# Six more products of a zero tile among the first value products of an mLSTM kernel

## The chip, the cores and the metric

The kernel runs on one core of a Trainium2 chip. The metric is the device time of one execution in microseconds (us). Three executions of the kernel before gave 563.04 us as median, from 562.67 to 563.28.

## The reference

Two parts follow each other. The first is an mLSTM recurrence over 768 positions for 4 batches and 8 heads of width 40, with an input gate, a forget gate, an output gate and a running maximum `m`:

```
m_new  = max(f[t] + m, i[t])
C      = exp(f[t] + m - m_new) * C + exp(i[t] - m_new) * outer(v[t], k[t])
n      = exp(f[t] + m - m_new) * n + exp(i[t] - m_new) * k[t]
y[t]   = sigmoid(o[t]) * (C @ q[t]) / max(|n . q[t]|, 1)
```

The second is a bilinear layer on the 3072 resulting rows of 320: `((y @ w_a) * (y @ w_b)) @ w_out`, with an inner width of 1536. The result is a float32 array of 3072 by 320.

## The kernel before, in words

The recurrence is computed in chunks of 128 positions. There are 24 pieces of attention work, 6 chunks for each of 4 batches; the program numbers them 0 to 23, and the numbers 0 to 3 are the first chunk of each batch. "Chunk 0" and "chunk 1" in the words on this change are the pieces 0 and 1. For one piece TensorE transposes q and k (L870), multiplies them (`pS`, L884), VectorE multiplies that by a matrix of decays (`gbc`, L890), TensorE multiplies the result by the values (`pV`, L927) and, for the state that the next chunk needs, weighted values by keys (`pU`, L628). VectorE then normalizes (`den`, `osig`, L669 to L680), TensorE transposes the result (`pX`, L707), and ScalarE and VectorE split it in a high and a low part, `xh` and `xl` (L711, L712). Those are the operands of the bilinear layer (`pu`, L810, and `pd`, L781), which is most of TensorE's work.

The weights arrive as 64 bit numbers and pass through 32 stages of preparation, each with a step on ScalarE (`signs`, L412), three on VectorE (`words`, L423, L424, L426), one on ScalarE (`leading`, L439), two small products (`pc`, L449 and L450) and one or two more steps on VectorE (`rests`, L457 or L455).

The opening of the kernel is written out by hand in `start()`, and every engine's order there is pinned to the order in which the code stands. From the end of `start()` on, a scheduler with its own timing model orders the instructions of each engine. In both parts each engine works its list off in order: an instruction that waits holds up all behind it on that engine.

In `start()` the function `busy(count)` issues `count` products of a tile of zeros, 128x336 in bf16 (L959), into a PSUM tile named `warm` that nobody reads. The opening has 13 of them at the very start, two at a time between the first steps, and groups of 4, 4, 4, 4 and 8 after the first update of the state. A function `dense` (L152) places three such products in front of the small products of the pieces 2 and 3. The groups after the state's update write a second tile, `warm2`, in the PSUM bank with the tag `pd2`; the first tile lies in the bank `pd1`, which the value product of piece 1 takes over.

Around the change, the order in `start()` is: the last product of the weights' stage 1 (`rests(1)`), `begin_c(0)` (the 8 heads' value products of piece 0), `weigh(0)` on GpSimd's side of the list, `signs(2)` on ScalarE, `begin_c(1)` (the value products of piece 1), `stage_f(0)`, `words(2)`, `stage_u(0)`.

Of the kernel before, what the change touches and what calls it, by code (L numbers as in the profile page):

```python
# [8 lines left out]
F32 = mybir.dt.float32  # L9
# [11 lines left out]
def kernel(  # L21
# [16 lines left out]
    P = 128  # L38
# [20 lines left out]
    ps_dn = ctx.enter_context(tc.tile_pool(name="ps_dn", bufs=1, space=PSUM))  # L59
# [89 lines left out]
    def dense(n, bank, count):  # L149
        if NS <= n < NE:  # L150
            for _ in range(count):
                nc.tensor.matmul(bank[:, 0:H * DV], zero[:, 0:P], zero, start=True, stop=True)  # L152
# [26 lines left out]
    def nat(n):  # L179
        return inner.get(n) or (qk[n % NQ], va[n % NQ])  # L180


    def load_qk(n):
        c, b = chunks[n]
        for j, x in enumerate((q, k)):
            issued["qk"[j], n] = nc.sync.dma_start(
                nat(n)[0][j][:, :, 0:D], x[b, :, c * P:(c + 1) * P, :].rearrange("h t d -> t h d")
            ).ins

    def load_v(n):  # L190
        c, b = chunks[n]
        nc.sync.dma_start(
            nat(n)[1][:, :, 0:D], v[b, :, c * P:(c + 1) * P, :].rearrange("h t d -> t h d")
        )

    def load(n):
        load_qk(n)
        load_v(n)
# [15 lines left out]
    def gate_o(c, bs=slice(0, B)):  # L214
        hot[0] = 3
        x = osig[c][:, bs, 0:DM]
        nc.scalar.activation(x, x, AF.Sigmoid)
# [16 lines left out]
    def gates_load():  # L234
        f, i = (apool.tile([P, S], F32, tag="pb", name=f"g_{x}")[0:BH] for x in "fi")
        nc.sync.dma_start(f, f_gate.rearrange("b h s -> (b h) s"))
        nc.scalar.dma_start(i, i_gate.rearrange("b h s -> (b h) s"))
        return f, i
# [136 lines left out]
    def fetch(to):  # L375
        while fetched[0] < min(to, len(stages)):
            x = fetched[0]
            fetched[0] += 1
            src = stages[x]
            n = src[0].shape[1]  # L380
            raw = rpool.tile([P, n], I64, tag=f"s{x}", name=f"raw{x}")
            r0 = 0
            for a in src:
                nc.sync.dma_start(raw[r0:r0 + a.shape[0]], a)
                r0 += a.shape[0]
            held[x] = [raw, n]
# [9 lines left out]
    def turn(j, x):  # L396

        if begun[j] > x:
            return False
        assert begun[j] == x  # L400
        begun[j] += 1
        return True

    def signs(x):
        if not turn(0, x):
            return
        raw, n = held[x]
        t = step[x % len(step)][:, :n]
        words = raw.bitcast(U32).rearrange("p (n w) -> p n w", w=2)
        held[x] += [t, words[:, :, 0]]  # L410
        with tc.issue_after(rounded[x - 2]) if x > 4 else nullcontext():
            nc.scalar.activation(  # L412
                t, words[:, :, 1].bitcast(F32), AF.Prelu, scale=2.0 ** -112, alpha=-(2.0 ** 32)
            )
# [16 lines left out]
    def leading(x):  # L431
        if not turn(2, x):
            return
        n, W, r = held[x]
        w = ws[x] = rpool.tile([P, 2, n], F32R, tag=f"s{x - 1}", name=f"w{x}")
        h = w[:, 0]
        if len(stages[x]) > 1:
            h = cpool.tile([P, WCH], F32R, tag="ct", name="ct", bufs=2)
        rounded[x] = nc.scalar.copy(h, W).ins  # L439
        held[x] += [w, h]  # L440

    def rests(x):
        leading(x)
        if not turn(3, x):
            return
        ready[0] = x + 1
        n, W, r, w, h = held.pop(x)
        pc = ps_up.tile([P, NTB], F32, tag="pu", name=f"pc{x}")[:, :n]
        nc.tensor.matmul(pc, eye[0], r, start=True, stop=False)  # L449
        nc.tensor.matmul(pc, eye[1], h, start=False, stop=True)  # L450
        if len(stages[x]) > 1:
            for j in range(2):
                rows, other = (slice(64 * i, 64 * i + 64) for i in (j, 1 - j))
                nc.scalar.copy(w[rows, j], W[rows])
                nc.vector.tensor_tensor(w[other, j], pc[rows], W[rows], op=ALU.add)  # L455
        else:
            nc.vector.tensor_tensor(w[:, 1], pc, W, op=ALU.add)  # L457
# [124 lines left out]
    def weigh(n):  # L582
        c, b = chunks[n]
        vw = apool.tile([P, H, DV], F32, tag="vw", name=f"vw{n}", bufs=1)
        nc.gpsimd.tensor_tensor(  # L585
            vw, nat(n)[1], w_col(c, b).unsqueeze(2).broadcast_to([P, H, DV]), op=ALU.mult
        )
        vws[n] = vw
# [326 lines left out]
    def begin_c(n):  # L915
        c, b = chunks[n]
        s = st[n]
        if n >= NS:
            weigh(n)
        if n < NS:  # L920
            pV = ps_dn.tile([P, 512], F32, tag=f"pd{min(n, 2)}", name=f"pV{n}")
        else:
            pV = ps_at.tile([P, 512], F32, tag="pat", name=f"pV{n}")
        pv = pV[:, 0:H * DV].rearrange("p (h d) -> p h d", h=H)
        dense(n, pV, 3)
        for h in range(H):
            nc.tensor.matmul(pv[:, h], s["E"][:, h, :], nat(n)[1][:, h], start=True, stop=True)  # L927
            if h % HH == HH - 1:
                yield
        if c > 0:  # L930
            nc.vector.tensor_tensor(s["num"], pv, s["num"], op=ALU.add)
        else:
            s["num"] = pv
        yield
# [14 lines left out]
    with tc.tile_pool(name="spool", bufs=3) as spool:  # L949

        def room(name):
            return spool.tile([P, H * P], F32, tag="x", name=name)

        def start():
            warm = ps_dn.tile([P, 512], F32, tag="pd1", name="warm")

            def busy(count):
                for _ in range(count):
                    nc.tensor.matmul(  # L959
                        warm[:, 0:H * DV], zero[:, 0:P], zero, start=True, stop=True  # L960
                    )

            def run(x, count=99):
                for _ in range(count):
                    if next(x, "end") == "end":
                        return

            busy(13)
            f, i = gates_load()
            load_qk(0)  # L970
            load_qk(1)
            fetch(2)
            load_v(0)
            load_v(1)
            fetch(3)
            load_o(0, (0, 1))
            fetch(5)
            load_qk(NS)
            load_o(0, (2, 3))
            fetch(6)  # L980
            load_v(NS)
            fetch(8)
            load(NS + 1)
            fetch(12)
            m0, w = gates_first(f, i)
            rest = gates_rest(f, i, m0)
            a0, e0, b0, e1, b1 = begin_a(0), begin_e(0), begin_b(0), begin_e(1), begin_b(1)
            run(a0, 1)
            busy(2)
            run(a0)  # L990
            busy(2)
            run(b0, 1)
            busy(2)
            run(rest, 1)
            signs(0)
            run(e0)
            words(0)
            run(begin_a(1))
            leading(0)
            signs(1)  # L1000
            run(b0)
            run(e1)
            gates_w(w)
            words(1)
            rests(0)
            run(b1)
            leading(1)
            gate_o(0, slice(0, 2))
            rests(1)
            run(begin_c(0))  # L1010
            weigh(0)
            signs(2)
            run(begin_c(1))
            run(stage_f(0))
            words(2)
            run(stage_u(0))
            load(NS + 2)
            weigh(1)
            leading(2)
            signs(3)  # L1020
            run(stage_f(1))
            d0, d1 = stage_d(0), stage_d(1)
            warm = ps_dn.tile([P, 512], F32, tag="pd2", name="warm2")
            busy(4)
            run(d0, 1)
            words(3)
            run(d0)
            leading(3)
            busy(4)
            rests(2)  # L1030
            signs(4)
            run(stage_u(1))
            fetch(18)
            load(NS + 3)
            fetch(26)
            busy(4)
            run(d1, 1)
            words(4)
            run(d1)
            leading(4)  # L1040
            busy(4)
            rests(3)
            busy(8)
            rests(4)
            signs(5)
            gate_o(0, slice(2, B))
            words(5)
            return rest

        with in_order():  # L1050
            rest = start()
# [66 lines left out]
```

## Time and profile before

| | |
|---|---|
| median of the executions timed | 563.04 us (562.67 to 563.28) |
| profiled execution: its own time | 560.51 us |
| its span, first to last instruction | 558.5 us |
| mean granted TensorE clock | 0.993 |
| busy: TensorE / VectorE / ScalarE / GpSimd | 544.9 / 389.4 / 267.9 / 126.9 us |

PE is TensorE's multiplying, PEld its loading of weights, DVE is VectorE, ACT ScalarE, POOL GpSimd and SP the queue that issues the transfers. A row of the timeline shows the start, the length up to the end of the last instruction merged in it, the engine, the line, the operation, the tiles and shapes and the number of instructions; in brackets stands how long the engine had been idle, and what ended that. Since matmuls are pipelined, the length of a row runs over the start of the next, and the time that a group takes is read from its start to the start of the next group. A fp32 product counts as two instructions. PEclk is the share of TensorE's full clock that was granted.

### The profile page before, as it was taken

To read this page: it belongs to the slowest core of one execution; us is meant where nothing else is said; L and a number is where in the kernel's file an instruction comes from. 1 tells how busy PE (TensorE), PEld (TensorE's weight loads), DVE (VectorE), ACT (ScalarE), POOL (GpSimd) and SP (SyncE) were. 2 spreads that over 40 slices of the span, in tenths; PEclk is the share of its full clock that TensorE was granted. 3 is DMA by queue.
4 is the path that set the end of the run, shared out by engine and by line. 5 is a ranking of instruction groups with operands and counts; after the bars stand their busy time and mean duration, and the time that the engine had idled before them with its cause. 6 is when DMAs were issued, how large, how long until landed. Compare 5 with 4: busy or idle time off the path is not lost.

```text
span 558.5 us, 12726 instructions
## 1 busy us (share of the span) xinstructions
PE 544.9 (98%) x4925; PEld 518.0 (93%) x4925; DVE 389.4 (70%) x888; ACT 267.9 (48%) x645; POOL 126.9 (23%) x188
## 2 busy tenths in 40 slices
PE   8999999899999999999999999999999999999997
PEld 6898898799999899999989999998999999999997
DVE  6889999964858683968749774977757755944332
ACT  5574678752626761556525654644526733310111
POOL 3102414641232320332031330333021302000000
PEclk9799999999999999999999999999999999999999
DMA  9999941393649762569536684586539704200001
GB/s 191 215 263 291 290 72 51 94 179 71 108 103 193 141 139 58 123 142 180 107 99 156 108 151 115 118 145 138 118 97 154 144 0 115 48 1 25 0 1 35
DMA packets 198551, 66.75 MB, mean 120 GB/s; under 512 B 184220, under 2 KB 191772, under 8 KB 198492
## 3 DMA queue, kind: packets, MB, share of 16 engines
q1 hardware_dynamic: 198444, 65.86, 56.4%
q8 instruction: 38, 0.62, 0.5%
q14 instruction: 21, 0.17, 0.1%
q10 hardware_dynamic: 48, 0.10, 0.0%
HBM read 41.11 MB, written 5.95 MB: 84 GB/s over the span
## 4 chain that ended last, share of the span: by engine, by line
PE 60%; DMA 17%; DVE 10%; ACT 5%; issue 3%; SPq 3%; POOL 1%; ACTq 0%; DVEq 0%; POOLq 0%
PE pu L810 31%; PE pd L781 15%; DMA T<-qks 4%; DMA c_dram<-cb 3%; ACT gbc L490 3%; DMA va<-in_v_dram 2%; PE pV L603 2%; PE pU L628 2%; DVE gbc L554 2%; DMA gbc<-g_dram 1%; DMA raw<-in_moe_w_a_dram 1%; DVE pb L556 1%; PE pS L884 1%; PE pV L927 1%; PE pS L545 1%
## 5 line engine op out<-in xcount | busy, mean ns | idle before, releaser
L810 PE MATMUL pu<-xh,w 128*128 128x384 f32 (+1 forms) x1080 | 276.5, 324 | 2.6 <-ACT g L816 0.9
L810 PE MATMUL pu<-xl,w 128*128 128x384 f32 (+1 forms) x648 | 208.0, 322 | 0.0
L810 PEld LDWEIGHTS pu<-xh,w 128*128 128x128 f32 x1080 | 190.6, 189 | 5.9 <-ACT g L816 1.3
L781 PE MATMUL pd<-w,gh 128*128 128x320 f32 x576 | 126.7, 309 | 0.0
L810 PEld LDWEIGHTS pu<-xl,w 128*128 128x128 f32 x648 | 122.2, 189 | 0.2
L817 DVE TENSOR_TENSOR g<-pu,g 128x384 f32<-128x384 f32 (+1 forms) x108 | 54.6, 505 | 89.4 <-PE pu L810 46.3
L781 PEld LDWEIGHTS pd<-w,gh 128*128 128x128 f32 x576 | 96.7, 188 | 0.1
L781 PE MATMUL pd<-w,gl 128*128 128x320 f32 x288 | 85.3, 310 | 0.0
L816 ACT COPY g<-pu 128x384 f32<-128x384 f32 (+1 forms) x90 | 39.6, 440 | 93.4 <-PE pu L810 84.2
L490 ACT ACTIVATE gbc<-gbc,gtab 128x128 f32<-128x128 f32 x160 | 49.1, 389 | 18.1 <-POOL gbc L483 18.0
L821 DVE TENSOR_TENSOR gl<-g,gh 128x384 fp32r<-128x384 f32 (+1 forms) x92 | 52.2, 568 | 1.9
L781 PEld LDWEIGHTS pd<-w,gl 128*128 128x128 f32 x288 | 53.1, 188 | 0.2
L585 POOL TENSOR_TENSOR vw<-va,gtab 128x336 f32<-128x336 f32 x20 | 16.4, 822 | 160.3 <-PE pU L628 135.2
L819 DVE CAST gh<-g 128x384 fp32r<-128x384 f32 (+1 forms) x108 | 41.1, 382 | 2.2
L483 POOL TENSOR_SCALAR_AFFINE_SELECT gbc<-gbc 128x1024 f32<-128x1024 f32 x20 | 22.6, 1132 | 65.1 <-DMA gbc<-g_dram 32.9
L554 DVE TENSOR_TENSOR gbc<-gbc,pb 128x512 f32<-128x512 f32 x36 | 27.2, 757 | 6.8 <-ACT pb L552 6.6
L603 PEld LDWEIGHTS <-pb 128*128 128x128 bf16 x576 | 23.4, 96 | 6.4 <-DVE pb L556 3.2
L684 POOL TENSOR_TENSOR osig<-osig,den 128x320 f32<-128x320 f32 x22 | 16.6, 754 | 54.9 <-DVE den L671 42.9
L603 PE MATMUL pV<-va,pb 128*128 128x42 bf16 x288 | 25.9, 183 | 2.7 <-DVE pb L556 2.7
L790 ACT COPY o<-pd 128x320 f32<-128x320 f32 x24 | 8.8, 434 | 40.3 <-PE pd L781 40.3
L550 DVE TENSOR_TENSOR gbc<-pS,gbc 128x512 f32<-128x512 f32 x36 | 23.7, 682 | 4.0 <-PE pS L545 4.0
L518 ACT COPY qks<-qks 128x640 bf16<-128x640 bf16 x36 | 26.0, 725 | 0.6
(154 smaller groups left out, 849.6 us busy)
## 6 DMA issues: line engine op xcount, KB each, us to landing
gbc<-g_dram SPq DMA_DIRECT2D x20, 512.0 KB
q<-in_q_dram SPq DMA_DIRECT2D x24, 160.0 KB
k<-in_k_dram SPq DMA_DIRECT2D x24, 160.0 KB
va<-in_v_dram SPq DMA_DIRECT2D x24, 160.0 KB
osig<-in_o_gate_dram SPq DMA_DIRECT2D x24, 160.0 KB
raw<-in_moe_w_out_dram SPq DMA_DIRECT2D x12, 320.0 KB
out_dram<-o SPq DMA_DIRECT2D x24, 160.0 KB
raw<-in_moe_w_a_dram SPq DMA_DIRECT2D x8, 384.0 KB
```

The source lines that it names most:

```text
L483: nc.gpsimd.affine_select(E, E, pattern=[[0, H], [1, P]], compare_op=ALU.is_ge, fill=-1e30, base=0, channel_multiplier=-1,)
L490: nc.scalar.activation(E[:, h], E[:, h], AF.Exp, bias=beta[:, h:h + 1])
L518: nc.scalar.copy(qks[:, 0, :, lo:lo + 2 * D], qks[:, 1, :, D - lo:3 * D - lo])
L550: nc.vector.tensor_tensor(E, pS, E, op=ALU.mult)
L554: nc.vector.tensor_tensor(E, E, pb[:, 0], op=ALU.subtract)
L603: nc.tensor.matmul(pv[:, h], pb[i][:, h % HH, :], vb[j][:, h], start=(x == 0), stop=(x == len(terms) - 1),)
L781: nc.tensor.matmul(pd[t][:, 0:DM], a[:, cols], w, start=(ff == 0 and first), stop=(ff == NF - 1 and last),)
L810: nc.tensor.matmul(acc[j], a, r, start=(x == 0), stop=(x == len(terms) - 1),)
L816: (nc.vector.tensor_copy if ff in [1, 2] else nc.scalar.copy)(g, acc[0])
L817: nc.vector.tensor_tensor(g, acc[1], g, op=ALU.mult)
L819: nc.vector.tensor_copy(gh, g)
L821: (nc.gpsimd if kb * 12 + ff < 16 else nc.vector).tensor_tensor(gl, g, gh.bitcast(F32), op=ALU.subtract)
```

## The change

The tile `warm2` is allocated earlier in `start()`, right after `rests(1)`. Two zero products are added in front of the value products of piece 0, and four between `signs(2)` and the value products of piece 1. All groups of zero products that were there stay.

```diff
@@ -1007,9 +1007,12 @@
             leading(1)
             gate_o(0, slice(0, 2))
             rests(1)
+            warm = ps_dn.tile([P, 512], F32, tag="pd2", name="warm2")
+            busy(2)
             run(begin_c(0))
             weigh(0)
             signs(2)
+            busy(4)
             run(begin_c(1))
             run(stage_f(0))
             words(2)
@@ -1020,7 +1023,6 @@
             signs(3)
             run(stage_f(1))
             d0, d1 = stage_d(0), stage_d(1)
-            warm = ps_dn.tile([P, 512], F32, tag="pd2", name="warm2")
             busy(4)
             run(d0, 1)
             words(3)
```

The first place is TensorE's list in `start()`, from the products of the weights' stage 1 (`pc`) to the state's update of piece 0 (`pU`). Before:

```order
L449 MATMUL pc_371<-cr,eye_80 128x384
L450 MATMUL pc_371<-w_368,eye_81 128x384
L927 MATMUL pV_375<-va_88,gbc_265 128x42 x8
L927 MATMUL pV_387<-va_89,gbc_317 128x42 x8
L628 MATMUL pU_407<-vw_384,k_85 64x42 x8
```

With the change (the two rows on `zero` and `warm_375` stand once for the first two products, and once for the four):

```order
L449 MATMUL pc_371<-cr,eye_80 128x384
L450 MATMUL pc_371<-w_368,eye_81 128x384
L959 LDWEIGHTS zero
L959 MATMUL warm_375<-zero 128x336
...
L927 MATMUL pV_378<-va_88,gbc_265 128x42 x8
L959 LDWEIGHTS zero
L959 MATMUL warm_375<-zero 128x336
...
L927 MATMUL pV_394<-va_89,gbc_317 128x42 x8
L628 MATMUL pU_414<-vw_387,k_85 64x42 x8
```

Nothing else moves in `start()`, on TensorE or on another engine. The scheduler's part stands as before at first, and from some 67 us of the span to some 155 us the engines' lists differ by places that were swapped. The second place is the first such swap on TensorE, around the products `pS` and `pI` of piece 5, which share two PSUM banks. Before:

```order
L450 MATMUL pc_982<-w_980,eye_81 128x320
L884 MATMUL pS_1_1121<-T_0_992,T_1_1012 128x128 x4
L449 MATMUL pc_1035<-cr,eye_80 128x384
L450 MATMUL pc_1035<-w_1033,eye_81 128x384
L781 MATMUL pd_0_578<-w_908,gh_3_938 128x320 x2
```

With the change:

```order
L450 MATMUL pc_988<-w_986,eye_81 128x320
L781 MATMUL pd_0_584<-w_914,gh_3_944 128x320 x2
L781 MATMUL pd_1_585<-w_914,gh_3_944 128x320 x2
L884 MATMUL pS_1_1127<-T_0_998,T_1_1018 128x128 x4
L904 MATMUL pI_0_1182<-cst_96,T_0_998 128x42 x4
L781 MATMUL pd_0_584<-w_914,gl_3_946 128x320
```

The first half of `pI`, which stood behind 16 products `pu` and four `pd` groups, now follows `pS` directly. VectorE's list moves with it: the multiplication L890, which empties the banks of `pS`, stands seven rows (first half) and three rows (second half) nearer to the front.

## The prediction

> **What bounds the kernel now.** I read the page first. TensorE is busy for 544.9 of 558.5 us, so what counts is how fast it works. One row of the 40 slices shows the only place where its clock gives way:
>
> ```profile
> PEclk9799999999999999999999999999999999999999
> ```
>
> The second slice (14 to 28 us) has 7 tenths. The view of windows finds the edges:
>
> ```profile
> 15.24:18.65 3.41, 3.41 (x33) 3.41 (x31) 2.86 (x9) 2.46 (x3) 0.00 (x0) 1.00 0.89 196
> 18.65:22.06 3.41, 3.41 (x26) 2.81 (x26) 3.20 (x10) 1.47 (x5) 0.75 (x1) 0.50 1.53 158
> 22.06:25.47 3.41, 3.41 (x24) 2.52 (x23) 2.69 (x7) 1.53 (x4) 0.00 (x0) 0.50 1.07 294
> 25.50:26.00 0.50, 0.50 (x7) 0.36 (x6) 0.47 (x2) 0.23 (x1) 0.13 (x1) 1.00 1.10 289
> ```
>
> Column three is PE, the number behind the last bracket is the clock. It is 1.00 up to 18.65, exactly half for 6.82 us, and full again. PE was never idle in it. The timeline of PE over that place, which is also the chain of waits there:
>
> ```profile
> 15.37 3.90 PE L927 MATMUL pV<-va,gbc 128*128 128x42 f32 x32
> 19.20 1.54 PE L628 MATMUL pU<-vw,k 128*64 128x42 f32 x16
> 20.67 1.30 PE L959 MATMUL warm<-zero 128*128 128x336 bf16 x4
> 21.77 0.85 PE L707 MATMUL pX<-ident,osig 128*128 128x128 f32 x3
> 22.41 1.33 PE L959 MATMUL warm<-zero 128*128 128x336 bf16 x4
> 23.32 0.73 PE L449 MATMUL pc<-cr,eye 128*128 128x384 f32 x1
> 23.85 0.52 PE L450 MATMUL pc<-w,eye 128*128 128x384 f32 x1
> 24.30 1.43 PE L628 MATMUL pU<-vw,k 128*64 128x42 f32 x16
> 25.66 0.74 PE L959 MATMUL warm<-zero 128*128 128x336 bf16 x4
> 26.24 0.49 PE L707 MATMUL pX<-ident,osig 128*128 128x128 f32 x3
> 26.57 0.73 PE L959 MATMUL warm<-zero 128*128 128x336 bf16 x4
> 27.02 0.45 PE L449 MATMUL pc<-cr,eye 128*128 128x384 f32 x1
> 27.32 0.34 PE L450 MATMUL pc<-w,eye 128*128 128x384 f32 x1
> 27.50 1.31 PE L959 MATMUL warm<-zero 128*128 128x336 bf16 x8
> 28.65 0.60 PE L870 MATMUL pT<-ident,q 128*128 128x128 f32 x4
> ```
>
> No row has a bracket: PE waits for nobody, its own work sets the pace. The clock falls after 3.3 us of value products, which stream only 42 columns each.
>
> **What the half clock costs.** The same operations at full clock, from start to next start, stand partly above and partly here:
>
> ```profile
> 40.38 1.88 PE L927 MATMUL pV<-va,gbc 128*128 128x42 f32 x16
> 42.09 0.36 PE L810 MATMUL pu<-xh,w 128*128 128x256 f32 x1
> 78.54 0.92 PE L628 MATMUL pU<-vw,k 128*64 128x42 f32 x16
> 79.39 0.38 PE L810 MATMUL pu<-xh,w 128*128 128x256 f32 x1
> ```
>
> pV x16 takes 1.71 and pU x16 0.85. A zero product takes 0.144 (eight from 27.50 to 28.65), the four of 25.66 took 0.58, pX 0.33 (26.24 to 26.57), pc 0.48 (27.02 to 27.50). Between 15.37 and 25.66 that makes, half clock against full: pV 3.83 against 3.42, pU 1.47 against 0.85, four zeros 1.10 against 0.58, pX 0.64 against 0.33, four zeros 0.91 against 0.58, pc 0.98 against 0.48, pU 1.36 against 0.85. The differences, 0.41, 0.62, 0.52, 0.31, 0.33, 0.50 and 0.51, sum to 3.20 us. The six added products cost 6 x 0.144 = 0.86 on the same path. Net -2.34: pT would start at 26.3 instead of 28.65.
>
> **Does the clock hold?** The trace does not show the new sequence, so I bound it by columns streamed in 3.41 us. From 15.24 to 18.65 PE ran 31 value products of 42 columns and one pc of 384, some 1690 columns, and the clock fell at the end. The poorest stretch that I found elsewhere in which it held is this one, the page's busy row and the part of it that is pV of a later piece:
>
> ```profile
> 189.31:192.72 3.41, 2.55 (x67) 2.34 (x66) 3.38 (x9) 1.66 (x4) 0.04 (x1) 1.00 0.77 173
> 189.31:192.72 3.41, 1.55 (x48) 1.34 (x48) 1.00 0.77 173
> ```
>
> 48 x 42 and, of the other 19, sixteen pU of 42 and about one pu of 384 make some 3070 columns, with PE idle for 0.86, at clock 1.00. In the changed kernel 15.24 to 18.65 holds the pc, six zeros (2016) and 2.41 us of value products at 0.107 (22 x 42), some 3320; the next 3.41 us hold eight zeros and the rest. That is above the stretch that held. If the 3.41 us were laid worst, with only four zeros in them, it is 1344 + 26 x 42 = 2440, half way between the two. So I take full clock as the value; both ends stay in the range: all of the 3.20 saved, or nothing of it.
>
> The Trainium skill, "TensorE: Matmul & The Clock Gate", section "What's actually happening", says that a monitor looks at how busy the array was in free-running windows of 3413 ns and passes full or half clock. The 6.82 us here are two of those. Its section on HAM oscillation asks for no idle gaps of over some 3 us; taken by that alone the clock would not have fallen here, where PE had no gap at all, and zeros would only cost their 0.86. The trace speaks against that reading.
>
> **What hides or stops the gain.** Earlier PE work must find its inputs. VectorE's rows in question:
>
> ```profile
> 17.29 0.17 DVE L669 TENSOR_SCALAR den<-pV 128x8 f32<-128x8 f32 x1 [0.36 <-PE pV L927]
> 21.33 0.64 DVE L680 TENSOR_TENSOR osig<-y,osig 128x320 f32<-128x320 f32 x1
> 22.77 0.56 DVE L426 SCALAR_TENSOR_TENSOR cr<-raw,qks 128x384 fp32r<-128x384 uint32 x1
> 24.41 0.56 DVE L457 TENSOR_TENSOR w<-pc,cw 128x384 fp32r<-128x384 f32 x1 [0.62 <-PE pc L450]
> 27.28 0.56 DVE L712 TENSOR_TENSOR xl<-pX,xh 128x384 fp32r<-128x384 f32 x1 [1.06 <-ACT xh L711]
> 29.64 1.14 DVE L455 TENSOR_TENSOR w<-pc,cw 64x384 fp32r<-64x384 f32 x2 [1.33 <-PE pc L450]
> 20.88 0.75 POOL L585 TENSOR_TENSOR vw<-va,gtab 128x336 f32<-128x336 f32 x1 [6.89 <-issue]
> ```
>
> The two zeros in front push `den` from 17.29 to 17.58, and with it `osig` of piece 1 to 22.26 and L426 of stage 3 to 23.62. PE would want them for the second pX at 23.9 and the second pc at 24.8: no wait. GpSimd's `vw` starts 0.14 after the first pU ends and takes 0.75; that pU now ends near 20.6, so `vw` is there at 21.5, and the second pU comes at 22.5. VectorE's three idle times, 0.62, 1.06 and 1.33, are waits for this PE work, directly or through `xh`: 3.01 less the 0.29 pushed leaves room for 2.7, more than the 2.34. Its L455 would start near 27.3.
>
> That start matters, because VectorE is then full:
>
> ```profile
> 30.00:108.00 78.00, 75.81 (x620) 68.02 (x619) 76.05 (x191) 53.63 (x134) 25.32 (x34) 1.00 0.69 178
> 103.95 0.39 PE L810 MATMUL pu<-xh,w 128*128 128x256 f32 x1 [0.67 <-DVE w L457]
> 105.88 0.41 PE L449 MATMUL pc<-cr,eye 128*128 128x320 f32 x1 [0.72 <-DVE cr L426]
> ```
>
> It is busy for 76.05 of 78 us, and at its end PE waits for it. A gain on PE alone would be eaten there; here both start 2.34 earlier. In the view of waits from 30 to 110 us VectorE waits for no transfer; this is its longest line there, the wait for pc from above:
>
> ```profile
> DVE w L455 <- PE pc L450: 1.3, 1, 1.3
> ```
>
> What could take some back is the new order near 67 us: the first half of pI comes right behind pS and needs the bank that L890 empties,
>
> ```profile
> 71.39 1.27 DVE L890 TENSOR_TENSOR gbc<-pS,gbc 128x512 f32<-128x512 f32 x2
> ```
>
> one of which takes 0.64. PE's wait for it lies between nothing and 0.64; I take the middle, 0.3. Allocating `warm2` earlier costs nothing: its bank was last written by the second transpose of piece 1, and ScalarE's copy of it is over by 12.1 us:
>
> ```profile
> 10.99 1.07 ACT L873 COPY T<-pT 128x512 f32<-128x512 f32 x2
> ```
>
> Sum: -3.20 + 0.86 + 0.3 = -2.0 us. The profiled execution, 560.51 (span 558.5), becomes 558.5 (span 556.5). It lies 2.5 below the median of the timed ones, which I cannot explain; I carry the difference over: 563.04 - 2.0 = 561.0.
>
> **The rivals.**
>
> (1) A shorter stretch. Where the edges of the clock's stretches lie against the program may differ from execution to execution; the profile shows one. If the half clock lasts 3.41 us instead of 6.82, the change has half as much to save: -1.60 + 0.86 = -0.74, 562.3. For it speaks that four zeros in the 3.41 us from 18.65 did not bring the clock back and four in the next did, so that where the edge lies decides; against it, the timed executions differ by 0.6 only, while such a mixture would spread them by 1.6. The Trainium skill's page (same section) calls these windows free-running, which is what this rival needs.
>
> (2) The zeros are too thin, and the clock falls all the same. Then nothing is saved, and the six products cost 0.86 at full clock, or 6 x 0.28 = 1.7 at half, as in this row of the opening (3.82 / 13 = 0.29):
>
> ```profile
> 1.10 3.82 PE L959 MATMUL warm<-zero 128*128 128x336 bf16 x13 [1.10 <-DVE zero L147]
> ```
>
> 563.9 to 564.7. It decides if the clock needs more than about 3320 columns in 3.41 us. Against it stands the stretch at 189 us.
>
> (3) The gain is there at 28 us and lost on the ramp, since the lists from 67 to 155 us differ. If PE's waits for VectorE at its end (0.67, 0.72) double and the wait for L890 is whole (0.64), -2.34 + 1.39 + 0.64 = -0.3: 562.7.
>
> **How the numbers follow.** Forecast 0.57, rival (1) 0.2, (2) 0.13, (3) 0.1. 0.2% is 1.1 us, about what a measurement of this kernel can tell from no change. The forecast is faster (0.57, and 0.01 of the rest), (1) and most of (3) are the same, together 0.27, (2) and a little of (3) are slower, 0.15. Low end: the timed executions, 2.5 slower than the profiled one, may lose one more stretch of 3.41 us at half clock there, 1.6; 561.0 - 1.6 = 559.4. High end: between (3) and the cheap end of (2), 563.6. The forecast's own range is 559.4 to 561.9.
>
> **What would show it.** Right: the clock is 1.00 in every window from 18 to 26 us, pT starts near 26.3 and L455 near 27.3, and PE's waits for VectorE near 104 us come some 2.3 earlier at their old length. Wrong: half clock anywhere between 18 and 26 (rivals 1, 2), or pT at 26.3 and the distance from there to the span's end longer than 529.8 by over 1 us (rival 3).

## The result, and the profile after

The change is slower: 564.14 us median (562.21 to 567.62, 20 executions) against 560.89 us (557.75 to 565.52, 20 executions of the kernel before). The ratio is 1.0068, 95% interval 1.0048 to 1.0087. Here and below a median is over all executions, while a ratio leaves out the slow ones, those more than 1.5% above the fastest of their kernel. The profiled execution took 562.21 us, its span is 560.3 us, its mean granted clock 0.991 (before: 560.51, 558.5, 0.993). It is the fastest of the twenty, so the median execution lost 1.9 us more than the rows below show.

The opening came out as forecast. The clock row of the profile's page, and below it the view of windows over the place where the half clock had been (columns as in the prediction: PE first, then PEld, DVE, ACT, POOL, the clock, the transfers' share and GB/s):

```profile
PEclk9999979999999999999999999999999999999999
```

```profile
15.24:18.65 3.41, 3.41 (x30) 3.07 (x30) 2.65 (x8) 2.47 (x3) 0.00 (x0) 1.00 1.04 211
18.65:22.06 3.41, 3.41 (x38) 3.04 (x38) 3.11 (x10) 1.42 (x4) 0.75 (x1) 1.00 1.45 163
22.06:25.47 3.41, 3.41 (x35) 2.59 (x33) 3.27 (x9) 2.54 (x8) 0.66 (x1) 1.00 1.07 303
```

Clock 1.00 in all three. The timelines of PE and of VectorE behind it:

```profile
26.48 0.60 PE L870 MATMUL pT<-ident,q 128*128 128x128 f32 x4
27.47 1.14 DVE L455 TENSOR_TENSOR w<-pc,cw 64x384 fp32r<-64x384 f32 x2 [0.43 <-PE pc L450]
```

`pT` starts at 26.48 instead of 28.65 and L455 at 27.47 instead of 29.64: both 2.17 us earlier. But the clock row has a 7 in its sixth slice (70 to 84 us) that was not there before. From `pT` to the span's end it is now 533.8 us, before 529.9: 4.0 us are lost on the way, and the loss begins at 65 us. The timeline of GpSimd with the change:

```profile
65.36 1.09 POOL L483 TENSOR_SCALAR_AFFINE_SELECT gbc<-gbc 128x1024 f32<-128x1024 f32 x1 [7.61 <-DMA gbc<-g_dram]
66.42 0.75 POOL L585 TENSOR_TENSOR vw<-va,gtab 128x336 f32<-128x336 f32 x1
67.12 0.72 POOL L684 TENSOR_TENSOR osig<-osig,den 128x320 f32<-128x320 f32 x1
```

and the same three operations in the kernel before:

```profile
63.17 0.75 POOL L585 TENSOR_TENSOR vw<-va,gtab 128x336 f32<-128x336 f32 x1 [3.23 <-PE pU L628]
64.33 0.73 POOL L684 TENSOR_TENSOR osig<-osig,den 128x320 f32<-128x320 f32 x1 [0.41 <-DVE den L671]
65.99 1.09 POOL L483 TENSOR_SCALAR_AFFINE_SELECT gbc<-gbc 128x1024 f32<-128x1024 f32 x1 [0.94 <-DMA gbc<-g_dram]
```

Before, GpSimd did the weighted values `vw` and the gated output `osig` of piece 3 first, and then the mask of piece 4 (L483), which needs a matrix `gbc` that a transfer brings. Now the mask stands first on its list. The transfer lands at about the same time in both (65 to 66 us), GpSimd stands 7.61 us for it, and `osig` comes at 67.12 instead of 64.33, although all else is 2 us ahead. VectorE waits for that `osig`, and TensorE for VectorE:

```profile
67.88 0.49 DVE L685 TENSOR_TENSOR osig<-pV,osig 128x320 f32<-128x320 f32 x1 [3.92 <-POOL osig L684]
```

```profile
64.64 0.75 PE L781 MATMUL pd<-w,gh 128*128 128x320 f32 x4
68.52 1.39 PE L884 MATMUL pS<-T,T 40*128 40x128 f32 x7 [3.13 <-DVE osig L685]
```

The windows show the price that comes on top of the wait:

```profile
65.52:69.00 3.48, 0.48 (x4) 0.52 (x5) 1.09 (x3) 2.52 (x9) 2.33 (x3) 1.00 1.00 267
69.00:72.41 3.41, 3.41 (x18) 3.33 (x18) 3.41 (x8) 3.41 (x12) 1.89 (x2) 0.50 0.34 63
72.41:75.83 3.42, 3.42 (x17) 3.42 (x16) 2.21 (x7) 3.22 (x11) 0.78 (x1) 0.50 0.02 5
96.31:99.72 3.41, 3.41 (x17) 3.37 (x17) 3.41 (x13) 1.41 (x4) 0.76 (x1) 0.50 0.00 0
```

PE works for 0.48 of 3.48 us, and the next 6.83 us are at half clock, and 3.41 more at 96 us. Where PE sets the pace, 10.24 us at half clock cost up to 5.1 us. With the wait of 3.13 that is more than the 4.0 lost from `pT` to the end; the kernel before has waits of its own for VectorE on this ramp, and no run separates the shares. The Trainium skill, "TensorE: Matmul & The Clock Gate", section "HAM oscillation — how this bites in real kernels", warns of idle gaps of over some 3.4 us; here a gap of 3.0 us was enough.

It is no chance of one execution. The mean granted clock of the 20 timed executions of the change lies between 0.981 and 0.991, its median at 0.989. Of the kernel before, the 120 executions timed beside the experiments have a median of 0.994, and single ones reach 1.000. Of a span of some 560 us, 0.005 is 2.8 us; the change lost 3.3 between the medians, 3.8 by the ratio (0.0068 x 560.9).

### The profile page after: what moved, and what is told of

Same layout as the page of the kernel before. It is cut to its first block, busy times and chain, and to the rows that moved or that the text cites. A ratio compares the mean times of both kernels' runs of the same rounds, so it can differ in the third digit from the quotient of the medians.

```text
span 560.3 us, 12732 instructions
## 1 busy us (share of the span) xinstructions
PE 543.8 (97%) x4931; PEld 519.8 (93%) x4931; DVE 386.6 (69%) x888; ACT 268.0 (48%) x645; POOL 126.5 (23%) x188
## 4 chain that ended last, share of the span: by engine, by line
PE 82%; DMA 6%; issue 4%; DVE 3%; ACT 2%; POOL 2%; ACTq 0%; SPq 0%; POOLq 0%; DVEq 0%
PE pu L810 43%; PE pd L781 20%; PE pV L603 4%; PE pU L628 3%; PE pS L545 2%; DMA gbc<-g_dram 2%; DMA T<-qks 2%; PE pS L884 1%; PE pX L707 1%; PE pV L927 1%; PE pI L571 1%; ACT gbc L490 1%; PE warm L959 1%; PE pT L870 1%; POOL gbc L483 1%
## 5 line engine op out<-in xcount | busy, mean ns | idle before, releaser
L819 DVE CAST gh<-g 128x384 fp32r<-128x384 f32 (+1 forms) x108 | 39.8, 368 | 2.2
L483 POOL TENSOR_SCALAR_AFFINE_SELECT gbc<-gbc 128x1024 f32<-128x1024 f32 x20 | 22.8, 1138 | 81.5 <-DMA gbc<-g_dram 48.4
```

Of the source, the lines that this page charges most:

```text
L483: nc.gpsimd.affine_select(E, E, pattern=[[0, H], [1, P]], compare_op=ALU.is_ge, fill=-1e30, base=0, channel_multiplier=-1,)
L819: nc.vector.tensor_copy(gh, g)
```

## The experiments

The theories, as the expectations number them. **A**: GpSimd's new order makes the loss. **B**: near 66 us a transfer sets the pace; whatever the opening gains is waited away there. **C** has two meanings: in e1 to e4 that the zeros cost TensorE more than they bring, from e5 on that the transfers as a whole are the limit. Later came **D** (small stores land late because they stand behind large loads in SP's queue), **F** (the one buffer of `cb` hands the stores' lateness on to ScalarE, and it to VectorE) and **G** (without that buffer another wait takes over). In the experiments' files lines past 350 can stand one to three higher than in the kernel before.

**Two or four of the zeros (e1_four, e2_two).** The first leaves out the two products in front of piece 0, the second the four between the pieces. With four alone every engine's list past the opening is that of the kernel before; with two alone it is that of the change.

```diff
# e1_four
-            busy(2)
             run(begin_c(0))
# e2_two
-            busy(4)
             run(begin_c(1))
```

> The four zero products between the value products of chunks 0 and 1 alone; the two in front are left out. From the end of the hand-written opening on, every engine's list is the one of the kernel before. Theory A (the loss comes from the scheduler's other lists, above all from GpSimd's, where the masking of the decays of piece 4, L483, now stands ahead of the weighting vw and the gate's product osig of piece 3 and holds them up until its transfer lands): the opening gains some 2 us here too and nothing is given back, 1.5 to 2.6 us faster than before, clock 1.00 from 18 to 26 us, no wait of TensorE over 1 us near 65 us. Theory B (whatever the opening gains is lost on a ramp that VectorE or the transfers bound, and the lists matter little): within 0.6 us of before. Theory C (zero products cost TensorE more than they bring): 0.5 to 1 us slower.

> The two zero products in front alone; the four are left out. From the opening on, every engine's list is the one of the changed kernel. Theory A: slower than before by 1 to 4 us, with L483 idle for some 7 us before it in GpSimd's list and the product pS of piece 4 waiting for osig near 66 us; the half clock from 18 to 25 us may be there as before. Theory B: within 0.6 us of before. Theory C: 0.3 us slower than before.

e1_four: 559.30 us against 558.44 (ratio 1.0009, 0.9984 to 1.0035), no difference that can be measured, where A had forecast a gain of 1.5 to 2.6 us. By the time alone C (0.5 to 1 us slower) would fit as well; the trace speaks against it, since `pT` starts at 25.91 us there, 2.74 ahead of the kernel before. e2_two: 562.74 us, 1.0070 (1.0031 to 1.0108), as slow as the change. So the two products in front, 0.29 us of TensorE's time, bring the loss, and it goes with the lists, not with the zeros' own time. But e1_four did not gain either, though its opening ran at full clock. Where its gain went, in three timelines of it, ScalarE, VectorE and TensorE:

```profile
67.82 0.33 ACT L646 CAST cb<-cst 128x168 bf16<-128x168 f32 x1 [6.37 <-DMA c_dram<-cb]
```

```profile
69.30 0.42 DVE L817 TENSOR_TENSOR g<-pu,g 128x256 f32<-128x256 f32 x1 [4.23 <-ACT g L816]
```

```profile
69.32 0.44 PE L449 MATMUL pc<-cr,eye 128*128 128x384 f32 x1 [3.32 <-ACT g L816]
```

ScalarE stands at the CAST that writes `cb` of piece 3 until the stores of `cb` of piece 2 have landed, since there is one buffer. The copy of `g` is behind it on ScalarE's list, and VectorE and TensorE wait for that.

**All six zeros with GpSimd's old order, and the new order without zeros (e3_repair, e4_forced).**

```diff
# e3_repair: the change, and
-        nc.gpsimd.affine_select(
+        with tc.issue_after(after["p"][0]) if n == 4 else nullcontext():
+            nc.gpsimd.affine_select(
...
-            for o in "BDEACUF":
+            for o in ("BDACUFE" if n == 3 else "BDEACUF"):
# e4_forced: the kernel before, and
-        nc.gpsimd.affine_select(
+        masked[n] = nc.gpsimd.affine_select(
...
-        nc.gpsimd.tensor_tensor(
+        with tc.issue_after(masked[4]) if n == 3 else nullcontext():
+          nc.gpsimd.tensor_tensor(
             vw, nat(n)[1], w_col(c, b).unsqueeze(2).broadcast_to([P, H, DV]), op=ALU.mult
```

> All six zero products, and one order added: the masking L483 of piece 4 has to be issued after osig (L684) of piece 3. With it GpSimd's list is that of the kernel before, and the other engines' lists differ from it in 14 rows. Theory A: 1.5 to 2.5 us faster than before, 4 to 6 us faster than the change. Theory B: slower than before or the same, since the order is not what costs. Theory C: 0.5 to 1 us slower than before.

> The kernel before without any added zero product, but the weighting vw of piece 3 has to be issued after the masking L483 of piece 4, so that GpSimd's list has L483 ahead of vw and osig as the changed kernel has. Theory A: the half clock from 18.6 to 25.5 us stays, and there is a wait of TensorE for osig near 67 us of 1 to 2 us (shorter than the 3.1 of the change, since TensorE comes there later and the transfer does not), with a second stretch of half clock if the wait is long enough: 1 to 5 us slower than before. Theories B and C: within 0.7 us of before.

e3_repair: 559.09 us against 558.44 (1.0020, 0.9998 to 1.0041); with the old order on GpSimd the loss is gone, though the gain of 1.5 to 2.5 us that A had forecast did not come. e4_forced: 566.14 us, 1.0123 (1.0080 to 1.0165); without a single added zero that order costs at least as much as the change did (the intervals just meet), and with 6.9 us more than the 1 to 5 that A had given it. Its view of waits names the same chain one step earlier:

```profile
PE pU L630 <- POOL vw L587: 2.7, 1, 2.7
```

That is A, for the loss. Neither run moves GpSimd's order alone: e3_repair has nearly all lists of the kernel before, and in e4_forced the scheduler placed several hundred of TensorE's 4,900 instructions anew. That it is GpSimd's order rests on the chain of waits, which stands in the change, in e2_two and in e4_forced and is missing in e3_repair. For the gain the windows of VectorE over the same six microseconds tell it, first of the kernel before, then of e3_repair:

```profile
64.00:70.00 6.00, 5.60 (x41) 5.08 (x41) 6.00 (x15) 3.96 (x14) 3.69 (x4) 1.00 0.88 224
```

```profile
64.00:70.00 6.00, 4.00 (x29) 3.62 (x30) 3.11 (x9) 3.06 (x11) 2.97 (x3) 1.00 1.04 282
```

VectorE was full before (6.00 of 6) and is idle for 2.89 of 6 us now: it arrives earlier and waits. ScalarE waited for the store in the kernel before too, only nobody missed it; before, and in e3_repair:

```profile
66.23 0.33 ACT L646 CAST cb<-cst 128x168 bf16<-128x168 f32 x1 [2.04 <-DMA c_dram<-cb]
```

```profile
66.94 0.33 ACT L647 CAST cb<-cst 128x168 bf16<-128x168 f32 x1 [5.04 <-DMA c_dram<-cb]
```

The store lands no earlier, however early the opening ends. In front of it on SP's list stands a load of `gbc` that waits for another store, `g_dram`; SP's waits, before and in e3_repair:

```profile
SPq L224 <- DMA g_dram<-gates_m: 1.6, 1, 1.6
```

```profile
SPq L224 <- DMA g_dram<-gates_m: 5.0, 1, 5.0
```

**The stores of `cb` ahead of that load (e5_six_cd, e6_before_cd), fewer zeros at the end (e7_const), both (e8_const_cd).**

```diff
# e5, e6, e8
-        return nc.sync.dma_start(t, g_dram[c - 1:c, b * H:(b + 1) * H, :].broadcast_to([P, H, P])).ins
+        with tc.issue_after(issued["c", NS]) if n == NE else nullcontext():
+            return nc.sync.dma_start(t, g_dram[c - 1:c, b * H:(b + 1) * H, :].broadcast_to([P, H, P])).ins
...
+                    u = stage_u(n)
+                    if n == NS:
+                        yield from u
                     if NE <= n + 2 < NCH:
                         load_g(n + 2)
-                    u = stage_u(n)
# e7, e8: the change, and
-            busy(8)
+            busy(2)
```

> The change's six zero products, with one edit more: the two pairs of stores of cb of piece 2 (c_dram<-cb) stand on SP's list ahead of the first load of gbc, which waits for g_dram to land. GpSimd's list is again that of before. Theory B (with the old lists the opening's gain is waited away at 66 us, because ScalarE stands at the CAST cb<-cst until the stores of c_dram have landed, and these stand on SP's list behind a load that waits 5.0 us for g_dram): the store is issued near 58 us, the CAST's wait falls from 5.0 us to under 2, PE's wait near 68 us (2.0) goes, and some 1.5 to 2 us are gained: ratio 0.996 to 0.998 against before. Rival C (the 16 transfer engines, busy throughout up to 66 us, set the pace, and the order on SP only chooses who waits): the wait turns up at the mask of gbc or at k, and the ratio is that of e3_repair, 1.000 to 1.004.

> The kernel before, without the six zeros, with the same edit of SP's list (the stores of cb of piece 2 ahead of the first load of gbc); the masks of gbc move by one place on GpSimd. Theory B: in the kernel before ScalarE waits there for 2.0 us and SP for g_dram only for 1.6, since the opening is 2.2 us slower; there is at most that to gain, and PE had little wait there: ratio 0.998 to 1.001, that is, over 1 us behind e5_six_cd. Rival C: 1.000 to 1.003, the same as e5_six_cd.

> The change's six zero products, and the last group of eight made two, so that the number of zeros is that of before; the opening ends 0.9 us sooner than with the change. GpSimd's list is that of before. Theory B: a still earlier PE waits longer at 66 us for the same store; nothing is gained: ratio 1.000 to 1.003, the CAST cb<-cst waits 5.5 us or more. The prediction's sum (what the opening gains is kept) would give -2.9 us, ratio 0.995.

> e7_const with the stores of cb ahead of the first load of gbc, as in e5_six_cd. Theory B: up to 0.9 us better than e5_six_cd, ratio 0.994 to 0.998. Rival C: 1.000 to 1.004.

Against 559.28 us of before: e5_six_cd 561.62 (1.0031, 1.0002 to 1.0060), e6_before_cd 560.82 (1.0027, 0.9994 to 1.0060), e7_const 556.91 (0.9975, 0.9941 to 1.0010), e8_const_cd 560.67 (1.0034, 1.0002 to 1.0067). The remedy of B failed: e5 and e8 are no better than e3_repair, and e5, e6 and e8 lie where C had put them (1.000 to 1.004). ScalarE in e5_six_cd:

```profile
66.02 0.33 ACT L647 CAST cb<-cst 128x168 bf16<-128x168 f32 x1 [6.87 <-DMA c_dram<-cb]
```

and the issue of its first two stores on SP, in e5_six_cd and then in e3_repair:

```profile
60.03 1.58 SPq L657 DMA_DIRECT2D c_dram<-cb  x2
```

```profile
62.02 0.70 SPq L657 DMA_DIRECT2D c_dram<-cb  x2
```

The stores were issued from 60.0 instead of 62.0 us, and the CAST could go on at 66.0 instead of 66.9: of 2 us earlier at the one end, 0.9 arrive at the other. TensorE waits for ScalarE behind it for 5.1 us, where it was 2.0 in e3_repair, and the clock is at half for 10.24 us from 66.46. B's guess that the order on SP's list is the cause falls; that the landing is what is waited for stands. e7_const is unclear by its interval; B had said nothing would be gained. The prediction's sum would have given 0.995 for it, and that is inside the interval too.

**The stores on another queue (e9 to e12).** ScalarE issues the store of `g_dram` and those of `cb` of piece 2 instead of SP: in the kernel before, in e1_four, in e7_const and in the change.

```diff
-        nc.sync.dma_start(g_dram.rearrange("c g t -> g c t"), G)
+        nc.scalar.dma_start(g_dram.rearrange("c g t -> g c t"), G)
...
+            eng = nc.scalar if n == NS else nc.sync
-            nc.sync.dma_start(cd[:, 3], cb[j * 64:j * 64 + D, 2])
-            nc.sync.dma_start(cd[:, 0:3], cb[j * 64:j * 64 + D])
+            eng.dma_start(cd[:, 3], cb[j * 64:j * 64 + D, 2])
+            eng.dma_start(cd[:, 0:3], cb[j * 64:j * 64 + D])
```

> The kernel before with five of its transfers (the store of g_dram and the four stores of cb of piece 2) issued by ScalarE instead of SP, so that they do not stand behind the weights' loads in SP's queue; no zeros added. Else the lists are those of before but for some 14 rows. Theory D (a small store lands only after the bulk loads that were issued ahead of it in the same queue: g_dram took 8.6 us and the stores of cb 4 to 5 us in e3_repair): g_dram lands in under 4 us, the stores of cb in under 3, the CAST cb<-cst waits no longer (2.0 us before). The time moves little, since PE of before was hardly waiting there: ratio 0.997 to 1.001. Rival C (the 16 engines are simply full, the queue does not matter): the stores take as long as before, ratio 1.000 to 1.003.

> The change's four zeros between the values' products of chunks 0 and 1 (without the two in front), and the same five transfers issued by ScalarE. GpSimd's list is that of before. Theory D: the gain of the opening (2 us and more) is kept: PE does not stand for 3.3 us at 66 us as in e1_four; ratio 0.994 to 0.997 against before, some 1.5 to 2 us better than e9_before_act. Rival C: PE waits at 66 us as in e1_four, ratio 1.000 to 1.003.

> e7_const (six zeros in front of and between the values' products, the last group of eight made two) with the same five transfers issued by ScalarE. Theory D: opening gain of some 3 us kept, ratio 0.992 to 0.996. Rival C: as e7_const, 0.996 to 1.001.

> The change itself, all lists as in it (the mask of gbc ahead of vw and osig of piece 3 on GpSimd too), but the same five transfers issued by ScalarE. Theory A with D (the change loses because on GpSimd's new list vw and osig stand behind a mask that waits 7.6 us for gbc, and gbc waits for g_dram in SP's queue): gbc lands some 3 to 5 us earlier, the mask's wait falls to under 4 us, PE's wait at pS (3.1) goes, and the ratio is 0.995 to 1.000 against before, where the change has 1.007. Rival (the loss comes from the other swaps of the new lists, on TensorE and VectorE): ratio 1.004 to 1.008 as with the change.

All four are slower by 2.4 to 3.0%: against 560.04 us, 573.77 (1.0264, 1.0199 to 1.0329), 577.95 (1.0297, 1.0236 to 1.0359), 578.18 (1.0238, 1.0164 to 1.0312) and 574.97 (1.0254, 1.0201 to 1.0307). They missed every expectation and tell nothing on D, because the edit made a larger wait of its own. ScalarE in e9_before_act:

```profile
54.08 0.32 ACTq L289 DMA_DIRECT2D g_dram<-gates_m  x1
54.45 0.60 ACT L849 ACTIVATE gbc<-pE 128x512 f32<-128x512 f32 x1 [17.01 <-DMA raw<-in_moe_w_b_dram]
```

The issue itself had to wait until 54.08, by the trace for a load of weights, and ScalarE stood in front of it for 17.01 us; TensorE waited 13.8 us behind ScalarE. In the kernel before SP issues it, with nothing behind it that computes:

```profile
52.69 0.34 SPq L289 DMA_DIRECT2D g_dram<-gates_m  x1
```

The Trainium skill, "DMA: Bandwidth & Descriptors", section "Issuing engines are not separate DMA queues", says that transfers of all issuing engines run on the same 16 engines and interleave, and that another issuer saves only the time of issuing. Whether a store from ScalarE lands sooner, no run here shows.

**Two buffers for `cb` (e13 to e16).** If the store cannot be made to land sooner, the wait for it can be taken away. In the kernel before, in e1_four, in e3_repair and in e7_const; room is made by keeping three small tiles of the opening in the second buffer.

```diff
-        cb = apool.tile([P, 3, HH, DV], BF16, tag="cb", name=f"cb{n}", bufs=1)
+        cb = apool.tile([P, 3, HH, DV], BF16, tag="cb", name=f"cb{n}", bufs=2)
...
-    place = wpool.tile([BH, BH // 2], F32, name="place")
-    sides = wpool.tile([BH, 2, 64], F32, name="sides")
+    spare = apool.tile([P, 3, HH, DV], BF16, tag="cb", name="cb_spare", bufs=2)
+    spare = spare.rearrange("p i h d -> p (i h d)").bitcast(F32)[0:BH]
+    place = spare[:, 0:BH // 2]
+    sides = spare[:, BH // 2:BH // 2 + 128].rearrange("p (a b) -> p a b", a=2)
+    ends = spare[:, BH // 2 + 128:][:, 0:(NC - 2) * BH // 2].rearrange("p (c x) -> p c x", c=NC - 2)
...
-        ends = wpool.tile([BH, NC - 2, BH // 2], F32, name="ends")
```

> The kernel before with two buffers for cb instead of one (room is made by keeping three small tiles of the opening in the second one until it is needed); no zeros added. The CAST cb<-cst of piece 3 then waits for no store of piece 2. Theory F (the one buffer of cb is the place where the opening's gain is lost: ScalarE stands at that CAST until the stores land, and VectorE and TensorE wait behind ScalarE): before waits 2.0 us there, but VectorE is busy for 6.00 of 6 us from 64 to 70, so nothing is to be had: ratio 0.998 to 1.002. Rival G (the place is set by the transfers as a whole, and other waits for them take over): the same here, 0.998 to 1.002.

> e13_before_cb2 with the four zeros between the values' products; all five lists are those of e13_before_cb2 but for the zeros. Theory F: ScalarE's wait of 6.4 us at the CAST and VectorE's 4.2 us behind it (as in e1_four) are gone, and 1 to 2 us of the opening's gain are kept: ratio 0.996 to 0.998, under e13_before_cb2 by 0.002 to 0.004. Rival G: VectorE waits as long at another place near 66 us (k, gbc), ratio as e13_before_cb2 within 0.001.

> e3_repair (all six zeros, the old list of GpSimd) with two buffers for cb. Theory F: the prediction's -2.0 us comes back, or most of it: ratio 0.996 to 0.998, where e3_repair had 1.002. Rival G: 1.000 to 1.004.

> e7_const (six zeros in front of and between the values' products, two instead of eight at the end) with two buffers for cb. Theory F: 0.9 us better than e15_six_cb2, ratio 0.994 to 0.997. Rival G: as e7_const, 0.996 to 1.001.

Against 559.68 us: e13_before_cb2 557.62 (0.9982, 0.9960 to 1.0004), e14_four_cb2 556.56 (0.9952, 0.9927 to 0.9977), e15_six_cb2 558.29 (0.9988, 0.9964 to 1.0011), e16_const_cb2 556.43 (0.9955, 0.9929 to 0.9981). e14 has the same lists as e13 but for the four zeros. In e14_four_cb2 the CAST of piece 3 is done at 55 us without a wait, and VectorE is busy for 5.05 of the six microseconds where it had 1.77 in e1_four; ScalarE and the windows of e14_four_cb2, then the windows of e1_four:

```profile
55.27 0.33 ACT L648 CAST cb<-cst 128x168 bf16<-128x168 f32 x1
```

```profile
64.00:70.00 6.00, 5.22 (x39) 4.71 (x38) 5.05 (x12) 3.00 (x11) 2.73 (x3) 1.00 0.79 205
```

```profile
64.00:70.00 6.00, 2.68 (x20) 2.29 (x19) 1.77 (x6) 2.18 (x7) 1.24 (x2) 0.99 1.00 291
```

The second buffer thus takes the wait away, and with the four zeros it is worth more than noise: e1_four had 1.0009 (0.9984 to 1.0035), e14_four_cb2 has 0.9952 (0.9927 to 0.9977). What the four zeros bring once the buffer is there is less sure. Between the medians of the ratios it is 0.0030 (0.9982 to 0.9952, some 1.7 us), inside F's 0.002 to 0.004, but the two intervals overlap, and 0.9952 itself lies below F's range. Nor was there much half clock left to remove: seven of the twelve executions of e13_before_cb2, without any added zero, have a mean clock of 0.999 or 1.000, against 11 of the 120 of the kernel before.

e16 came out inside F's range, e15 above it (0.996 to 0.998) and below G's. In e15_six_cb2 another wait takes over, as G had it: TensorE stands 2.60 us for GpSimd's `gl` at 71.51 us, where it is 1.11 in e14_four_cb2, and the clock is at half for 3.41 us from 71.17; VectorE then waits 2.3 us for `pc`. Where the longer wait comes from was not followed further.

**The change with two buffers, and e14 once more (e17_change_cb2, e18_four_cb2_again).** The edit is the one above.

> The change itself with two buffers for cb and nothing else; on GpSimd the mask of gbc stands ahead of vw and osig of piece 3, as in the change. Theories A and F together (GpSimd's order makes the loss, by a wait for gbc that has nothing to do with cb; the one buffer of cb only eats the gain): PE still waits some 3 us at pS near 66 us, the clock falls behind it, and the ratio stays at 1.003 to 1.007 against before, 0.004 or more over e15_six_cb2, which differs by the old GpSimd order. Rival (the buffer of cb explains both): 0.996 to 1.000.

> e14_four_cb2 once more, beside e17 on one chip. Theory F: ratio 0.993 to 0.998 again. If e14's 0.9952 was luck of the clock's stretches, 0.998 to 1.002.

Against 559.36 us: e17_change_cb2 567.27 (1.0142, 1.0100 to 1.0184), e18_four_cb2_again 556.85 (0.9966, 0.9940 to 0.9992). The buffer does not cure the change: GpSimd's wait and TensorE's wait behind it are there as before, over twice as dear as A and F had said (1.003 to 1.007), with the clock at half for 17.06 us behind them. GpSimd, PE and the windows of e17_change_cb2:

```profile
65.25 1.09 POOL L485 TENSOR_SCALAR_AFFINE_SELECT gbc<-gbc 128x1024 f32<-128x1024 f32 x1 [7.50 <-DMA gbc<-g_dram]
```

```profile
68.41 1.42 PE L886 MATMUL pS<-T,T 40*128 40x128 f32 x8 [3.03 <-DVE osig L687]
```

```profile
69.10:86.16 17.06, 15.54 (x62) 14.39 (x62) 10.46 (x28) 8.45 (x25) 3.38 (x4) 0.50 0.28 55
```

So there are two causes: the new lists, by GpSimd's order, make the loss; the wait for the one buffer of `cb` takes the gain. Four zeros, GpSimd's old order and two buffers beat the kernel before in both runs, and by their ratios the change too. Against e13_before_cb2 (0.9982) the second run gives the four zeros 0.0016, half of what the first gave, and again the intervals overlap.

## Why the prediction was wrong

Two steps failed: the gain was taken as kept behind the opening, and the new lists were priced at +0.3 us. The first takes the gain away, the second turns it into a loss.

- **The half clock and its price at 28 us: right for that execution.** Forecast -2.34, measured -2.17 for `pT`; L455 forecast near 27.3, measured 27.47. The clock is 1.00 from 14 to 26 us in the profiles of all 14 kernels here that have four or six of the zeros. The inputs of the opening came in time too (no brackets in PE's rows).
- **"A gain on PE alone would be eaten there; here both start 2.34 earlier": the step that failed for the gain.** I counted two engines and took it that, if PE and VectorE start earlier, they end earlier. The transfers did not come earlier. With one buffer for `cb`, ScalarE's CAST goes on at 66.23 us in the kernel before, 66.94 in e3_repair and 67.82 in e1_four; SP can issue the load of `gbc` at 59.30, 61.12 and 62.07. I had read that "from 30 to 110 us VectorE waits for no transfer"; it waits for engines that wait for transfers. The trace of before showed it: 2.04 us on ScalarE for the store, 1.6 on SP for `g_dram`, and a transfers' share of 0.88 from 64 to 70 us. These waits cost nothing as long as VectorE was busy for 6.00 of those 6 us. What it came to: e1_four and e3_repair, with the opening's gain and without GpSimd's new order, are at 1.0009 and 1.0020 of before.
- **"What could take some back is the new order near 67 us", +0.3: the step that turned the gain into a loss.** I priced one swap of `pI` and `pS`, and on the ramp I looked at TensorE and VectorE alone. In the change `pI` has no wait at all. What counted stood on GpSimd's list, where an operation that needs a transfer was moved in front of two that VectorE needs. Price: from `pT` to the end +4.0 us, where I had +0.3.
- **Rival (3)** had the right place, the ramp, and too low a price: it counted waits (+2.0) and not that a wait of 3 us on PE takes the clock with it.
- **Rival (1) was there too.** Four more profiles have an opening without added zeros. In e6_before_cd the half clock lasts from 18.56 to 25.38 us as in before, in e13_before_cb2 and e4_forced only 3.41 us (from 18.81 and from 19.12), in e9_before_act there is none in the opening, and `pT` starts at 28.49, 27.16, 27.15 and 26.66. The row of e13_before_cb2:

```profile
27.16 0.60 PE L872 MATMUL pT<-ident,q 128*128 128x128 f32 x4
```

Against that row the change's `pT`, at 26.48, is 0.68 us earlier, close to rival (1)'s -0.74. That the forecast met 2.17 is thus partly luck: the one profile that I had showed the long stretch.
- **The yardstick of the clock, columns per 3.41 us, does not hold.** By the same count e9_before_act has some 2000 columns from 17.10 to 20.52 us and keeps clock 1.00 behind them; e1_four has some 2800 from 83.47 to 86.89, with PE busy throughout, and the next 3.41 us are at half clock. The stretch at 189 us was also one of bf16 products, where those of the opening are fp32. That the zeros hold the clock came true, but this reason for it is not shown.
- **The offset to the median.** I carried over 2.5 us "which I cannot explain", and held against rival (1) that the timed executions differ by 0.6 only. There were three. Twenty of the same kernel spread over 7.8 us. Nine of the 120 executions of the kernel before had a mean clock of 1.000, so no half clock in the opening either; their median is 557.54 us, the median of all 559.25. Even a whole opening at full clock came with some 1.7 us, not 3.20.

Open is why two zeros in front and not the four between move the mask ahead on GpSimd's list; the lists show that it is so, not why the scheduler did it. Open, too, are whether e7_const gains by itself and what exactly takes the clock.

## What to carry to other kernels

Before an opening is made faster, look at what the engines further on wait for, on every engine and the queue too, a wait of an engine nobody misses included: an earlier arrival turns such slack into a stall. When a scheduler orders the rest, compare all engines' lists, those of the lightly used ones first; an operation that waits for a transfer, moved in front of others on an in-order engine, passes its wait on to them, and if TensorE stands for it, the clock can go as well (here behind a wait of 3.13 us). And three executions say little about a spread, one profile little about where the clock's stretches lie.

## What the runs showed that I had not expected

The granted clock differs between executions of one program: 0.981 to 1.000 as the mean over the span, for the same instructions. All but one of the 120 executions of the kernel before lie between 555.25 and 564.26 us, 1.6% apart. The clock is a part of that only: the nine at 1.000 still go from 556.28 to 559.27. The Trainium skill, "TensorE: Matmul & The Clock Gate", section "What's actually happening", says that the windows are free-running and that the effect varies from run to run; the runs agree. It puts the cost of the ramp at under 1% of a typical span. That is the start; here half clock also stood between 66 and 100 us, and in e13_before_cb2 at 380.6 us.

The length of an idle gap alone does not tell whether the clock goes. In e7_const TensorE was idle for 1.50 of the 3.41 us up to 67.85, and the clock fell; in e3_repair it was idle for 1.65 of the 3.41 us up to 70.20, and the clock stayed. The windows, first of e7_const, then of e3_repair:

```profile
64.44:67.85 3.41, 1.91 (x15) 1.52 (x13) 0.98 (x4) 0.57 (x2) 0.28 (x1) 1.00 0.82 234
67.85:71.26 3.41, 3.32 (x13) 3.32 (x14) 2.80 (x8) 2.60 (x11) 1.91 (x2) 0.50 0.96 239
```

```profile
66.79:70.20 3.41, 1.76 (x13) 1.76 (x14) 1.78 (x4) 3.26 (x11) 1.83 (x2) 1.00 0.97 239
70.20:73.61 3.41, 3.41 (x30) 3.22 (x28) 3.41 (x9) 3.41 (x12) 0.86 (x2) 1.00 0.01 3
```

The issue of a transfer can hold up a computing engine for 17.01 us (e9_before_act), although the transfer that it issues is 80 KB.
